# Zeros beside the last 64 keys' values, and two heads in every step, in a top-k attention, feed-forward and expert kernel

## The chip, the cores and the metric

The kernel runs on one NeuronCore of a Trainium2 chip. The metric is device time in microseconds (us): the median of several executions, beside one execution that the hardware profiler recorded. The engines are TensorE (PE; its weight loads are listed as PEld), VectorE (DVE), ScalarE (ACT), GpSimd (POOL) and SyncE (SP, which issues most DMAs).

## What is computed

Three layers, one after the other. The attention has 4 batches, 8 heads, 576 keys and head size 64; of each row of scores the 32 largest are kept. Its output, 2304 tokens of 512 values, passes a gated feed-forward layer (width 1536) and then a layer of 8 experts (width 1024), where every token goes to one expert.

```python
scores = scale * np.matmul(q, k.transpose(0, 1, 3, 2))
kth = np.partition(scores, -top_k, axis=-1)[..., -top_k:-top_k + 1]
scores = np.where(scores >= kth, scores, -1000000000.0)
attn = np.exp(scores - np.max(scores, axis=-1, keepdims=True))
attn = attn / (np.sum(attn, axis=-1, keepdims=True) + 1e-09)
x = np.matmul(attn, v)                        # heads side by side: 2304 x 512
xn = x / rms * rms_g                          # the feed-forward layer
x = silu(xn @ w_gate) * (xn @ w_val) @ w_out
out[mask] = gate_w[mask] * (relu(x[mask] @ w1[e]) @ w2[e])   # the experts
```

## The kernel before

**Tiles and steps.** The 576 queries and keys of a head are four chunks of 128 and a remainder of 64 (`SM` is 512, `SR` is 64). A tile is 128 rows of queries against all 576 keys: a main tile is one chunk of one head, a remainder tile holds 64 queries each of two heads. With 8 heads, 4 batches, 4 chunks and the remainders that is 128 main tiles and 16 remainder tiles. Two tiles make a step, and `main_steps` (L78) and `rem_steps` (L87) say which two; there are 72 steps. `PLAN` (L93) lists the chunks in order; only its entry `[0, 1]`, for the third batch, makes steps of two chunks.

**The path of a tile.** `dma_q`, `split_q` and `trans_q` bring in the queries: each value is split into a high and a low part on POOL (L456, L457), transposed on PE (L465) and copied to `qS`. `dma_k`, `split_k`, `trans_k` do the same for keys, once for a pair of heads, into `kS`. `qk` (L521) forms the scores on PE (L530); ACT copies them (L543); `topk` finds the 32nd largest on DVE with MAX8 and MATCH_REPLACE8 (L565, L568), after DVE has split each row into pairwise maxima and minima (L545, L546). `soft0` to `soft3` make the exponentials on POOL and ACT (L586, L595, L599, L603). `tr` (L616) transposes them on PE (L625) into `pT`; for the two tiles' last 64 keys together one more transpose (L630) makes `pr`, whose rows 0 to 63 belong to the step's first tile and rows 64 to 127 to its second.

**Values.** `dma_v` (L381) loads a pair of heads into `vt`: four chunks of 128 rows, and the last 64 keys twice, into the upper and the lower half of the rows (L388). `split_v` makes two 16-bit parts of it, `vs`, on ACT, DVE and POOL (L394 to L396). Of the first batch's second half of heads (`WHOLE`) the values stay 32-bit. `av` (L651) multiplies on PE (L671). A main tile in 16 bits takes 12 products with 128 rows (four chunks, three products each: high by high, high by low, low by high) and then 3 with 64 rows, the half of `pr` and of `vt` that belongs to this tile (`r0`). A remainder tile goes through this twice, once for each head in it, with 64 columns of exponentials each (12 products of 128 rows by 64 columns, then 3 of 64 by 64). ACT writes the result, scaled, to `xn` (L680).

```python
            r0 = i % 2 * SR
            parts = [(0, 128, hh)] if hh is not None else [(0, 64, 0), (64, 64, 1)]
            for o, n, h2 in parts:
                    ks = slice(0, 128) if c2 < CM else slice(r0, r0 + SR)
                nc.tensor.matmul(out=av_[o:o + n], lhsT=l, rhs=r, ...)
```

**The feed-forward layer** is cut into granules, one per 128 tokens (one granule has 256). A granule's matmuls are all at L750: 288 products into `pf` (gate and value half) and 72 into `po`, 6192 in all. `mlp_slot` (L1012) puts them, a few atoms at a time, into the seven slots of each attention step, so that PE has work while the attention waits; what is left over follows after the last step.

**The order on each engine** is fixed when the program is built: a scheduler in the framework places the instructions of the code above, with a priority for `tr`, `av` and `qk` (L1061 to L1067), and each engine then runs its list in order. The experts (L1109 on) begin after the last granule.

## Time and profile before

| what | value |
|---|---|
| median of 3 runs | 1242.8 us (1239.47 to 1243.44) |
| the profiled execution's own time | 1240.91 us |
| its span | 1239.3 us |
| PE busy | 1138.8 us, 92% |
| PEld busy | 1039.9 us, 84% |
| DVE busy | 928.2 us, 75% |
| ACT busy | 830.5 us, 67% |
| POOL busy | 731.2 us, 59% |
| mean granted TensorE clock | 0.937 |

All rows are from the profiled execution. The profiler models the end of a matmul, so matmuls overlap in it and a busy share of PE near 100% says only that no gap was long; how fast products follow each other is read from the starts of neighbouring rows. The attention's steps run from about 45 us to 833 us, the rest of the feed-forward layer to 928 us, the experts to the end.

### The profile page before, as it was taken

The page shows a single profiled execution, that of the slowest core. Times are in us where ns is not written, and L with a number is a line of the kernel's source. Part 1 is how long each engine was busy: PE and PEld are TensorE (multiplying, and loading weights), DVE is VectorE, ACT ScalarE, POOL GpSimd, SP SyncE. Part 2 cuts the span into 40 slices and gives each one's busy share as a digit, 9 for nine tenths or more (in the row PEclk, how much of TensorE's full clock was granted, in tenths as well). Part 3 has the DMA queues.
Part 4 walks back from the last instruction along what each step waited for, and adds up shares of the span by engine and source line. Part 5 has one row for each costly group of instructions (what it writes and reads, how often), then busy time and mean ns, then how long its engine had stood idle before and what let it go on. Part 6 is the DMA issues. An engine that isn't in the chain of part 4 may idle for free. (4 is left out here: it accounts for less than half of the span.)

```text
span 1239.3 us, 32187 instructions
## 1 busy us (share of the span) xinstructions
PE 1138.8 (92%) x12286; PEld 1039.9 (84%) x12286; DVE 928.2 (75%) x2886; ACT 830.5 (67%) x1757; POOL 731.2 (59%) x843
## 2 busy tenths in 40 slices
PE   6976677999999999999999999999997999999994
PEld 6965566888999989999998999999986898798883
DVE  8999999759999999998999999971125526244161
ACT  6868888777888888878888887873333435344260
POOL 7866766858767879867889676564434312222100
PEclk9865676989999999999999999999997999999997
DMA  8242312011000111000011000013006726354230
GB/s 295 51 129 82 100 44 82 13 45 39 21 17 9 32 41 47 24 13 15 17 38 40 28 17 2 11 32 124 11 19 193 247 70 230 128 173 149 66 113 20
DMA packets 69624, 87.54 MB, mean 71 GB/s; under 512 B 34626, under 2 KB 43974, under 8 KB 69448
## 3 DMA queue, kind: packets, MB, share of 16 engines
q1 hardware_dynamic: 62360, 67.86, 17.9%
q0 software_dynamic: 5424, 13.16, 3.3%
q10 hardware_dynamic: 1664, 4.19, 0.9%
q8 instruction: 107, 1.75, 0.6%
q14 instruction: 69, 0.57, 0.2%
HBM read 75.58 MB, written 10.92 MB: 70 GB/s over the span
## 5 line engine op out<-in xcount | busy, mean ns | idle before, releaser
L565 DVE MAX8 w<-w 128x8 f32<-128x296 f32 x576 | 251.9, 462 | 1.2
L599 POOL TENSOR_TENSOR s<-s,r 128x576 f32<-128x576 f32 x144 | 201.1, 1417 | 31.3 <-ACT r L595 31.1
L568 DVE MATCH_REPLACE8 w<-w 128x296 f32<-128x296 f32 x432 | 194.9, 455 | 0.0
L750 PE MATMUL pf<-xT,wg 128*128 128x128 f16 (+1 forms) x2448 | 172.0, 224 | 4.2 <-DVE T L879 2.6
L750 PE MATMUL pf<-xT,wv 128*128 128x128 f16 (+1 forms) x2448 | 167.7, 222 | 0.0
L750 PE MATMUL po<-wo,h 128*128 128x264 f16 (+1 forms) x1296 | 157.4, 275 | 0.9 <-ACT t L777 0.9
L530 PE MATMUL ps<-kS,qS 128*128 128x288 f32 x640 | 138.6, 346 | 20.7 <-DVE w L546 19.6
L750 PEld LDWEIGHTS <-wg 128*128 128x128 f16 x2448 | 148.3, 99 | 11.1 <-issue 4.9
L750 PEld LDWEIGHTS <-wv 128*128 128x128 f16 x2448 | 145.3, 98 | 4.3
L750 PEld LDWEIGHTS <-h 128*128 128x128 f16 x1296 | 122.0, 98 | 18.8 <-issue 1.4
L1137 DVE TENSOR_TENSOR wl<-wr,wh 128x1024 fp32r<-128x1024 f32 x64 | 76.7, 1220 | 66.1 <-ACT wh L1136 66.1
L530 PEld LDWEIGHTS ps<-kS,qS 128*128 128x128 f32 x640 | 104.0, 215 | 23.8 <-ACT r L595 14.9
L603 ACT ACTIVATE s<-s,mbs 128x576 f32<-128x576 f32 x144 | 113.3, 789 | 14.2 <-POOL s L599 13.9
L595 ACT ACTIVATE r<-s,mbs 128x576 f32<-128x576 f32 x144 | 105.0, 781 | 15.1 <-POOL mbs L586 15.0
L625 PE MATMUL pt<-identr,s 128*128 128x128 f32 x576 | 97.6, 300 | 16.9 <-ACT s L603 16.1
L543 ACT COPY s<-ps 128x576 f32<-128x576 f32 x144 | 93.1, 646 | 22.1 <-PE ps L530 21.5
L1243 POOL DMA_INDIRECT out_dram<-o,idx x23 | 23.2, 1010 | 138.0 <-ACT o L1242 106.9
L1184 PE MATMUL ph<-xh,wh 128*128 128x256 f32 x352 | 99.7, 287 | 1.0 <-PEq L1301 1.0
L1184 PE MATMUL ph<-xl,wh 128*128 128x256 f32 x352 | 98.5, 282 | 0.0
L1184 PE MATMUL ph<-xh,wl 128*128 128x256 f32 x352 | 97.1, 284 | 0.8 <-issue 0.8
L782 POOL TENSOR_TENSOR t<-u,t 128x512 f32<-128x512 f32 x54 | 69.6, 1289 | 47.9 <-ACT t L777 30.3
L671 PE MATMUL pt<-vs,pT 128*128 128x64 f16 (+1 forms) x1680 | 88.4, 198 | 8.7 <-POOL pT L639 6.7
(205 smaller groups left out, 2779.0 us busy)
## 6 DMA issues: line engine op xcount, KB each, us to landing
wr<-in_moe_w_dram SPq DMA_DIRECT2D x56, 512.0 KB
wst<-in_moe_w_gate_dram SPq DMA_DIRECT2D x24, 256.0 KB
wst<-in_moe_w_val_dram SPq DMA_DIRECT2D x24, 256.0 KB
kr<-in_k_dram SPq DMA_DIRECT2D x32, 128.0 KB
vt<-in_v_dram SPq DMA_DIRECT2D x32, 128.0 KB
x_d<-xo SPq DMA_DIRECT2D x16, 256.0 KB
wr<-in_moe_w_dram ACTq DMA_DIRECT2D x8, 512.0 KB
qr<-in_q_dram SPq DMA_DIRECT2D x112, 32.0 KB
```

Source lines behind the costliest of these rows:

```text
L530: nc.tensor.matmul(out=ps[:, a, 0:HS], lhsT=qS[i // 2][:, i % 2, j, o2:o2 + 128], rhs=kt[:, m, ks], start=(n == 0), stop=(n == len(ops) - 1),)
L543: nc.scalar.copy(out=s.rearrange("p (a k) -> p a k", a=2), in_=ps[:, :, 0:HS])
L565: steps.append(lambda: dve.max(lists[t][:, 8 * r:8 * r + 8], src[t] if r == 0 else dst[t]))
L568: steps.append(lambda: dve.match_replace(out=dst[t], in_to_replace=lists[t][:, 8 * r:8 * r + 8], in_values=src[t] if r == 0 else dst[t], i ...
L595: nc.scalar.activation(out=d["r"], in_=d["s"], func=AF.Relu, scale=-BIG, bias=d["mb"][:, 1:2])
L599: nc.gpsimd.tensor_tensor(out=d["s"], in0=d["s"], in1=d.pop("r"), op=OP.subtract)
L603: nc.scalar.activation(out=d["s"], in_=d["s"], func=AF.Exp, scale=SCALE, bias=d["mb"][:, 0:1], accum_out=d["rs"])
L625: nc.tensor.transpose(pt[:, c * 128:(c + 1) * 128], e[:, e0 + c * 128:e0 + (c + 1) * 128], ident)
L671: nc.tensor.matmul(out=av_[o:o + n], lhsT=l, rhs=r, start=(a == 0), stop=(a == len(ops) - 1))
L750: nc.tensor.matmul(out=out_, lhsT=l, rhs=r, start=(a == 0), stop=(a == len(ops) - 1))
L1137: nc.vector.tensor_tensor(out=lo, in0=w[0], in1=hi.bitcast(F32), op=OP.subtract)
L1184: nc.tensor.matmul(out=pt, lhsT=l[:, fs], rhs=r[:, kk, :], start=(n == 0), stop=(n == 3 * KD - 1))
```

## The change

- `dma_v` loads the last 64 keys of the pair's first head into rows 0 to 63 and of its second head into rows 64 to 127, once each; a POOL memset writes zeros into the other half (two memsets of 64x64 for each of 16 pairs; 32 DMAs of 64 for the last keys go).
- `av` uses all 128 rows for the last keys too: the other tile's rows of `pr` meet zeros. It also uses all 128 columns for a remainder tile, once per head, into two column ranges of the result (`m * D`), of which half the rows are read. The number of products stays.
- So that zeros meet the other tile, a step's two tiles must be the two heads of a pair. `main_steps` now makes steps so for the entry `[0, 1]` too (its eight steps' queries come in two DMAs in place of one), and a remainder tile now holds every second head: tile `hh` of a step has heads `2p + hh` and `2(p + 1) + hh`. `qk` takes the keys from two pairs for it.

```diff
@@ main_steps, rem_steps
-            if len(cs) == 2:
-                for hh in range(2):
-                    steps.append([(b, p, hh, c) for c in cs])
-            else:
-                steps.append([(b, p, hh, cs[0]) for hh in range(2)])
+            for c in cs:
+                steps.append([(b, p, hh, c) for hh in range(2)])
...
-            steps.append([(b, p, None, None), (b, p + 1, None, None)])
+            steps.append([(b, p, None, hh) for hh in range(2)])
@@ dma_v
+                nc.gpsimd.memset(vt[(1 - i) * SR:(2 - i) * SR, i, CM, :], 0.0)
                 nc.sync.dma_start(out=vt[:, i, 0:CM, :], in_=v[b, h, 0:SM, :].rearrange("(p c) d -> p c d", c=CM))
-                for j in range(2):
-                    nc.sync.dma_start(out=vt[j * SR:(j + 1) * SR, i, CM, :], in_=v[b, h, SM:S, :])
+                nc.sync.dma_start(out=vt[i * SR:(i + 1) * SR, i, CM, :], in_=v[b, h, SM:S, :])
@@ dma_q
-            if hh is not None and t1[2] == hh:
-                src = q[b, 2 * p + hh, 0:SM, :].rearrange("(p c) d -> p c d", c=CM)
-                nc.sync.dma_start(out=qr, in_=src[:, c:c + 2, :])
...
+                        nc.sync.dma_start(out=qr[i * SR:(i + 1) * SR, t, :], in_=q[b, 2 * (p + i) + c, SM:S, :])
@@ qk
-                ops = [(o2, m, j) for o2, m in ([(0, hh)] if hh is not None else [(0, 0), (64, 1)]) for j in range(2)]
+                ks_ = [(0, kS[b, p][:, hh, ks])] if hh is not None else [(64 * m, kS[b, p + m][:, c, ks]) for m in range(2)]
+                ops = [(o2, kt, j) for o2, kt in ks_ for j in range(2)]
@@ av
-            r0 = i % 2 * SR
...
-            parts = [(0, 128, hh)] if hh is not None else [(0, 64, 0), (64, 64, 1)]
+            parts = [(0, 128, p, hh)] if hh is not None else [(64 * m, 64, p + m, c) for m in range(2)]
...
-                    ks = slice(0, 128) if c2 < CM else slice(r0, r0 + SR)
-                    src, q0 = (pT, c2 * 128 + o) if c2 < CM else (pr, o)
-                    e = [src[ks, a, q0:q0 + n] for a in range(nh)]
+                    e = [pT[:, a, c2 * 128:(c2 + 1) * 128] if c2 < CM else pr[:, a] for a in range(nh)]
...
-                    nc.tensor.matmul(out=av_[o:o + n], lhsT=l, rhs=r, start=(a == 0), stop=(a == len(ops) - 1))
+                    nc.tensor.matmul(
+                        out=d["pt"][:, m * D:(m + 1) * D], lhsT=l, rhs=r, start=(a == 0), stop=(a == len(ops) - 1)
+                    )
```

The scheduler places everything anew, so rows move on all engines. Six lines fewer stand in the changed file, so L750 is L744 there, L671 is L663, L530 is L524, L625 is L619, L639 is L633.

On PE, where the second group of 48 feed-forward products (L750 before, L744 now; `wv` are the value half's weights) stands among the scores (`ps`), some 40 tiles into the program. Before:

```order
L530 MATMUL ps<-kS,qS 128x288 x8
L625 MATMUL pt<-identr,s 128x128 x4
L630 MATMUL sm<-identr,s 128x128
L425 MATMUL pk<-identr,ks 128x128
L671 MATMUL pt<-vt,pT 128x64 x8
L671 MATMUL pt<-vt,pr 128x64 x2
L465 MATMUL pq<-identr,qs 128x128 x4
L530 MATMUL ps<-kS,qS 128x288 x4
L421 MATMUL pk<-identr,ks 128x128 x4
L750 LDWEIGHTS wv_110
L750 MATMUL pf<-xT,wv_110 128x128
```

Now:

```order
L524 MATMUL ps<-kS,qS 128x288 x8
L619 MATMUL pt<-identr,s 128x128 x4
L421 MATMUL pk<-identr,ks 128x128 x4
L744 LDWEIGHTS wv_110
L744 MATMUL pf<-xT,wv_110 128x128
```

The feed-forward products stand ahead of one tile's scores and of one tile's products with the values that they followed before. The distance grows a little: by the 45th tile's scores 541 of the 6192 products at L744 have been listed, where 409 at L750 had been; at the last tile's scores it is 4832 and 4680; behind the last product with the values 1128 follow, where 1304 did (864 into `pf` in place of 1016, 264 into `po` in place of 288).

On PE, a remainder tile of the first batch among its products with the values. Before:

```order
L671 MATMUL pt<-vt,pr 64x64
L671 MATMUL pt<-vt,pT 64x64 x4
L671 MATMUL pt<-vt,pr 64x64 x2
L671 MATMUL pt<-vt,pT 64x64 x4
L671 MATMUL pt<-vt,pr 64x64
L425 MATMUL pk<-identr,ks 128x128
```

Now:

```order
L663 MATMUL pt<-vt,pr 128x64
L663 MATMUL pt<-vt,pT 128x64 x4
L663 MATMUL pt<-vt,pr 128x64 x2
L663 MATMUL pt<-vt,pT 128x64 x4
L663 MATMUL pt<-vt,pr 128x64
L524 MATMUL ps<-kS,qS 128x288 x4
```

The same number of products stands there, each now writing 128 rows of the result.

On POOL, early in the attention, where the scores minus the threshold (`s`), the splits of queries (`qs`) and values (`vs`) and the low parts of the exponentials (`pT`) follow each other. Before:

```order
L609 TENSOR_SCALAR sums<-sums 128x2
L639 TENSOR_TENSOR pT<-pf,pT 128x512
L586 TENSOR_TENSOR mbs<-w,cst_66 128x6
L639 TENSOR_TENSOR pT<-pf,pT 128x512
L599 TENSOR_TENSOR s<-s,r 128x576 x2
L456 TENSOR_TENSOR qs<-qr,zero 128x2x128
L396 TENSOR_TENSOR vs<-vt,vs 128x640
```

Now:

```order
L603 TENSOR_SCALAR sums<-sums 128x2
L386 MEMSET vt 64x64 x2
L633 TENSOR_TENSOR pT<-pf,pT 128x512
L580 TENSOR_TENSOR mbs<-w,cst_66 128x6
L633 TENSOR_TENSOR pT<-pf,pT 128x512
L593 TENSOR_TENSOR s<-s,r 128x576 x2
L396 TENSOR_TENSOR vs<-vt,vs 128x640
```

Two memsets of a pair's values stand in POOL's line, a few instructions ahead of the split that reads them.

## Rows read from the trace of the kernel before

**Rows 1.** The page: busy time by engine, and 40 equal slices of the span, in tenths.

```profile
PE 1138.8 (92%) x12286; PEld 1039.9 (84%) x12286; DVE 928.2 (75%) x2886; ACT 830.5 (67%) x1757; POOL 731.2 (59%) x843
...
DVE  8999999759999999998999999971125526244161
...
PEclk9865676989999999999999999999997999999997
```

**Rows 2.** Stretches: start:end, length, busy (count) by engine, granted clock, DMA share, GB/s.

```profile
60.00:150.00 90.00, 63.44 (x385) 54.29 (x385) 89.96 (x300) 70.87 (x150) 63.24 (x73) 0.61 0.37 105
150.00:280.00 130.00, 108.67 (x1072) 97.16 (x1072) 108.74 (x368) 102.15 (x227) 91.16 (x105) 0.81 0.17 47
280.00:833.50 553.50, 547.95 (x7435) 507.06 (x7433) 529.04 (x1803) 459.39 (x1026) 422.84 (x491) 1.00 0.09 24
833.50:927.50 94.00, 91.55 (x1328) 86.76 (x1327) 18.09 (x99) 30.01 (x60) 35.90 (x35) 1.00 0.15 50
927.50:1239.30 311.80, 280.17 (x1770) 249.08 (x1770) 130.85 (x191) 125.32 (x211) 68.94 (x70) 0.95 0.42 139
```

**Rows 3.** PE's longest waits, 280 to 833.5: total us, times, longest us.

```profile
PE pf L750 <- DVE u L772: 1.2, 1, 1.2
PE pf L750 <- DVE T L879: 1.0, 2, 0.6
```

**Rows 4.** DVE's longest wait in the same stretch.

```profile
DVE w L545 <- ACT s L543: 5.8, 14, 1.2
```

**Rows 5.** PE in order of time around a main tile: start, us, instruction, count.

```profile
412.79 0.72 PE L750 MATMUL pf<-xT,wg 128*128 128x128 f16 x10
413.35 0.51 PE L671 MATMUL pt<-vs,pT 128*128 128x64 f16 x12
413.80 0.26 PE L671 MATMUL pt<-vs,pr 64*128 64x64 f16 x3
413.99 0.29 PE L750 MATMUL pf<-xT,wg 128*128 128x128 f16 x2
```

**Rows 6.** Stretches, the matmuls of L671 alone: busy and count on PE, PEld.

```profile
280.00:833.50 553.50, 93.76 (x1770) 76.09 (x1770) 1.00 0.09 24
```

**Rows 7.** PE in order of time around a remainder tile.

```profile
371.55 0.57 PE L671 MATMUL pt<-vs,pT 128*64 128x64 f16 x12
372.05 0.28 PE L671 MATMUL pt<-vs,pr 64*64 64x64 f16 x3
372.25 0.56 PE L671 MATMUL pt<-vs,pT 128*64 128x64 f16 x12
372.75 0.28 PE L671 MATMUL pt<-vs,pr 64*64 64x64 f16 x3
372.96 0.40 PE L750 MATMUL pf<-xT,wg 128*128 128x128 f16 x4
```

**Rows 8.** PE in order of time: the last step's tiles, mixed, and a later feed-forward atom.

```profile
832.98 0.20 PE L671 MATMUL pt<-vs,pr 64*128 64x64 f16 x1
833.11 0.20 PE L671 MATMUL pt<-vs,pT 128*128 128x64 f16 x1
...
842.85 8.14 PE L750 MATMUL po<-wo,h 128*128 128x264 f16 x72 [0.30 <-ACT t L777]
```

**Rows 9.** A stretch with the clock low, and in it PE's feed-forward products.

```profile
257.00:268.00 11.00, 10.56 (x80) 9.14 (x81) 9.30 (x27) 9.46 (x24) 5.61 (x8) 0.54 0.22 60
...
264.65 3.64 PE L750 MATMUL pf<-xT,wg 128*128 128x128 f16 x32
```

**Rows 10.** POOL's memsets by form: count, busy us, mean ns, idle before.

```profile
L476 POOL MEMSET qS<- 128x256 f32 x8 | 2.5, 317 | 3.7 <-PE ps L530 3.7
...
L204 POOL MEMSET acc_oh<- 128x8 f16 x1 | 0.1, 105 | 0.1
```

**Rows 11.** SP's issues of the last keys' values (ns min/median/max), and a wait of SP.

```profile
L388 SPq DMA_DIRECT2D vt<-in_v_dram x64: 465/588/1630, 45.6 to 679.6; - x64
...
SPq L445 <- POOL qs L457: 128.9, 25, 11.1
```

More of the change, by code (lines that the diff above doesn't have):

```diff
@@ L435, in dma_q @@
             qr = ap_.tile([128, 2, D], F32, name="qr", tag="qr", bufs=QB)
-            t0, t1 = steps[s]
-            b, p, hh, c = t0
-            if hh is not None and t1[2] == hh:
-                src = q[b, 2 * p + hh, 0:SM, :].rearrange("(p c) d -> p c d", c=CM)
-                nc.sync.dma_start(out=qr, in_=src[:, c:c + 2, :])
-            else:
-                for t, (b, p, hh, c) in enumerate(steps[s]):
-                    if hh is not None:
-                        src = q[b, 2 * p + hh, 0:SM, :].rearrange("(p c) d -> p c d", c=CM)
-                        nc.sync.dma_start(out=qr[:, t, :], in_=src[:, c, :])
-                    else:
-                        for i in range(2):
-                            nc.sync.dma_start(out=qr[i * SR:(i + 1) * SR, t, :], in_=q[b, 2 * p + i, SM:S, :])
+            for t, (b, p, hh, c) in enumerate(steps[s]):
+                if hh is not None:
+                    src = q[b, 2 * p + hh, 0:SM, :].rearrange("(p c) d -> p c d", c=CM)
+                    nc.sync.dma_start(out=qr[:, t, :], in_=src[:, c, :])
+                else:
+                    for i in range(2):
+                        nc.sync.dma_start(out=qr[i * SR:(i + 1) * SR, t, :], in_=q[b, 2 * (p + i) + c, SM:S, :])
             raw["q", s] = qr
@@ L523, in qk @@
             ps = ps_s.tile([128, 2, 512], F32, name="ps", tag="s")
-            kt = kS[b, p]
             for a in range(2):
@@ L653, in av @@
             d = st[i]
-            pT, pr, av_ = d["pT"], d["pr"], d["pt"][:, 0:D]
-            r0 = i % 2 * SR
-            vt = vS[b, p]
+            pT, pr = d["pT"], d["pr"]
             nh = 1 if whole(b, p) else 2
-            parts = [(0, 128, hh)] if hh is not None else [(0, 64, 0), (64, 64, 1)]
-            for o, n, h2 in parts:
+            parts = [(0, 128, p, hh)] if hh is not None else [(64 * m, 64, p + m, c) for m in range(2)]
+            for m, (_, _, p2, h2) in enumerate(parts):
+                vt = vS[b, p2]
                 ops = []
                 for c2 in range(CM + 1):
-                    ks = slice(0, 128) if c2 < CM else slice(r0, r0 + SR)
-                    src, q0 = (pT, c2 * 128 + o) if c2 < CM else (pr, o)
-                    e = [src[ks, a, q0:q0 + n] for a in range(nh)]
+                    e = [pT[:, a, c2 * 128:(c2 + 1) * 128] if c2 < CM else pr[:, a] for a in range(nh)]
                     if nh == 1:
-                        ops.append((e[0], vt[ks, h2, c2, :]))
+                        ops.append((e[0], vt[:, h2, c2, :]))
                     else:
-                        w = [vt[ks, a, h2, c2, :] for a in range(nh)]
+                        w = [vt[:, a, h2, c2, :] for a in range(nh)]
                         ops += [(e[0], w[0]), (e[0], w[1]), (e[1], w[0])]
                 for a, (l, r) in enumerate(ops):
-                    nc.tensor.matmul(out=av_[o:o + n], lhsT=l, rhs=r, start=(a == 0), stop=(a == len(ops) - 1))
+                    nc.tensor.matmul(
+                        out=d["pt"][:, m * D:(m + 1) * D], lhsT=l, rhs=r, start=(a == 0), stop=(a == len(ops) - 1)
+                    )
             blk, x0 = (b * CM + c, 0) if hh is not None else (NMB + b // 2, (b % 2) * SR)
@@ L677, in post @@
             def post():
-                for o, n, h2 in parts:
-                    hd = 2 * p + h2
+                for m, (o, n, p2, h2) in enumerate(parts):
+                    hd = 2 * p2 + h2
                     nc.scalar.activation(
-                        out=x[x0:x0 + n, hd * D:(hd + 1) * D], in_=av_[o:o + n], func=AF.Copy,
+                        out=x[x0:x0 + n, hd * D:(hd + 1) * D], in_=d["pt"][o:o + n, m * D:(m + 1) * D], func=AF.Copy,
                         scale=d["rs"][o:o + n],
```

4 lines of the change are left out of this document (2 added, 2 removed).

## The prediction

> **What bounds the kernel now.** I read the page first, then a table of stretches, then the waits of PE and DVE in the longest of them, and at last PE's rows in order of time. PE is busiest over the whole run, but the slices of DVE are at 9 or more for most of the first two thirds and fall behind [rows 1]; so the run has parts with different limits. The table [rows 2] has five.
>
> - 60 to 150: DVE is busy 89.96 of 90.00 us. It is the bound; PE waits.
> - 150 to 280: DVE 108.74 and PE 108.67 of 130.00, at a granted clock of 0.81 on the mean. Neither is full.
> - 280 to 833.5: DVE 529.04 of 553.50, and the clock at its full level of 2.4 GHz (1.00). PE's longest wait here for anything is 1.2 us, its second 1.0 [rows 3], so PE issues practically all the time and bounds this stretch. DVE's 24.5 idle us are short waits for work that hangs on PE: the longest sum is 5.8 us in 14 pieces, for the copies of the scores [rows 4].
> - 833.5 to 927.5: feed-forward products alone. DVE is busy 18.09 of 94.00; PE is the bound.
> - The experts, 311.80 us, which the change does not touch.
>
> **The change part by part.**
>
> *The change of rows on PE.* Around a main tile the 12 products with 128 rows start at 413.35 and last 0.51 us in all. One alone is listed with 0.20 [rows 8], so eleven intervals take 0.31 to 0.32 (the rows are rounded) and one 0.029 us. At that pace the first product with 64 rows would start at 413.70; it starts at 413.80. The three with 64 rows last 0.26, so they too follow each other by about 0.03, the next other product would start at 413.89, and it starts at 413.99 [rows 5]. Each change between 128 and 64 rows thus costs 0.10 us, and two of them are in every tile: 0.64 us from the first product to the next instruction, where 15 x 0.029 = 0.44 would do. I take 0.20 us a main tile. A remainder tile runs from 371.55 to 372.96, 1.41 us, with 30 products that need 0.87 at the same pace; it saves 0.54 [rows 7]. In 280 to 833.5 there are 1770 products with the values [rows 6]; twelve remainder tiles (three batches' worth, of four) have 360 of them and the rest makes 94 main tiles: 94 x 0.20 + 12 x 0.54 = 25.3 us. The scheduler also mixes tiles, so that one product with 64 rows stands between others with 128 (832.98, 833.11 [rows 8]), each such piece paying both changes again. In the built order before, the products with the last keys stand in 209 separate runs, where unmixed tiles would have 160 (128 + 2 x 16). With a third more runs than tiles the sum is 25.3 x 209 / 160 = 33 us of PE's time in this stretch, which the new form doesn't need: all its products have 128 rows and columns.
>
> *What that is worth.* PE's need there falls from about 548 to about 515 us, while DVE's 529.04 busy us stay. Behind PE, DVE is next, and the stretch can shrink by 24.5 us at most; at least by nothing, if DVE's short waits are latencies of the chain and not PE's fault. In 60 to 150 DVE shows that it can run without a gap [rows 2], which speaks for the upper end; the copies it waits for also wait on ACT, busy 459.39, which speaks for the lower. I take the middle: **-12 us**, ends -24 and 0.
>
> *Feed-forward products ahead.* In the new order 1128 instead of 1304 feed-forward products stand behind the last product with the values. That is 152 fewer into `pf` and 24 fewer into `po`. In `pf` ten take 0.72 us and two 0.29, so eight intervals take 0.43 and one 0.054 us [rows 5]; in `po` 72 take 8.14, 0.111 each [rows 8]. The stretch behind the attention loses 152 x 0.054 + 24 x 0.111 = 8.2 + 2.7 = **-11 us**. These products were not saved but moved; 132 of them stand ahead of the 45th tile's scores already, that is before 280 us. There PE has 130.00 - 108.67 = 21 us free in 150 to 280 [rows 2]. 132 x 0.054 = 7.1 us fit in at the full clock; at the lower level of 1.2 GHz 32 products take 3.64 us, about 0.11 each [rows 9], and the 132 need 14.5. I take 0 for this stretch, with ends at -5 (row changes go here as well) and +15 (the products come ahead of scores that DVE waits for).
>
> *The memsets.* There are 32 of 64x64. Between the smallest, 105 ns for 128x8, and 317 ns for 128x256 [rows 10] I take 0.2 us, 6.4 us in all. They read nothing, so POOL doesn't wait in them, and POOL is busy 422.84 of 553.50 [rows 2]: it hides them. Without that cover they stand ahead of the threshold subtractions and cost up to 6.4 us. I take 0.
>
> *DMAs.* 32 of the 64 loads of last keys go, at 588 ns of SP's time each; eight loads of queries come. SP itself waits 128.9 us for POOL to free query buffers [rows 11], so its queue is ahead of need. Nothing. The remainder's scores need keys of two pairs at once; all pairs of a batch are loaded in its first four steps. Nothing. ACT's copies keep their number.
>
> The sum is -12 - 11 = -23 us. Against the profiled execution's 1240.9 that is 1218; the median of the runs stands 1.9 us above that execution, so I name **1219 us**.
>
> **A rule against the change.** The three products with 64 rows follow each other by about 0.03 us, as those with 128 rows do [rows 5]; two of them do not run at once. The sum above hence gives nothing up with them. The Trainium skill, "TensorEngine Tiling (Array Packing)", section Performance Considerations, recommends the opposite of this edit: for a contraction of 64 rows, tile the array twofold, since tiles work in parallel. By that rule two neighbouring tiles' last products would share their time and the edit would give up half of it. From the rows that is 0.03 x 3 / 2 = 0.045 us a main tile, about 5 us over 94 main tiles, and the time would be 1224. No row shows the overlap, so it stays inside the range.
>
> **The rivals.**
>
> 1. *DVE is a wall.* Its waits are latencies, the stretch 280 to 833.5 stays as long as it is although PE is freed, and only the shorter rest behind the attention counts: -11, **1231 us**. For it: DVE is busy 96% there [rows 2]. Against it: no idle time at all in 60 to 150. Chance 0.2.
> 2. *DVE closes up.* All of its 24.5 us go, and the early stretch gives its 5: -24 - 11 - 5 = -40, **1202 us**. For it: PE hardly waits [rows 3]. Against it: the mixture of latencies in DVE's waits. Chance 0.1.
> 3. *Slower: the early feed-forward products block the attention.* The 132 products run at the low clock ahead of scores, +15, and the memsets delay the threshold subtractions, +6; DVE, with only 24 us of slack in the whole rest, can't take that back, and the rest behind the attention is 11 shorter: +10, **1252 us**. It decides from the point where the early delay exceeds what the later stretches give back. For it: in 150 to 280, with the clock at 0.81, DVE is idle for 21 us and so already waits for others [rows 2]. Against it: PE has as much idle time there. Chance 0.07.
> 4. *The row count is not what costs.* If the 0.10 us come with the change of operands (from `pT` to `pr`), they stay, PE remains the bound to the end, and work moved ahead only changes place: **1242 us**, within 4. Against it: in rows 5 the next `pf` product pays the same on the way back, though it shares nothing with `pr`, and the change from `pf` to `pT` is free: ten times 0.054 after 412.79 is 413.33, and `pT` starts at 413.35. Chance 0.08.
>
> **How the numbers follow.** The forecast has 0.55. Its own range is 1209 to 1230. A measurement of this kernel can tell 0.3%, 3.7 us, from no change. Forecast and rivals 1 and 2 are all below 1239: faster 0.85. Rival 4 is the same: 0.08. Rival 3 is slower: 0.07. The range reaches from rival 2 to near rival 4, 1202 to 1238; outside lie half of rival 4 and rival 3, and something of the edges.
>
> **What would show it.** In the profile after, no product of `av` has 64 rows or columns, and from the first of a main tile's 15 products to the next instruction it takes 0.44 us and not 0.64. In the table of stretches PE has waits again between 280 us and the attention's end, on DVE's work, and DVE's share there rises above 96%. The attention ends about 12 us earlier, near 821, and some 83 us of feed-forward products follow where 94 did. If the 0.64 stays, the step on rows is wrong; if it falls and the attention ends at 833, rival 1; if the early stretch to the 45th tile is longer by over 10 us, rival 3.

## The result and the profile after

The median of the changed kernel is **1228.65 us** (1226.30 to 1230.71, 4 runs) against 1241.13 us for the kernel before in the same runs: a ratio of 0.9898, with a 95% interval of 0.987 to 0.9926. It is faster by 12.5 us. The forecast was 1219, with a range of 1202 to 1238: direction and range hold, and about half of the expected gain is there. The profiled execution after took 1229.35 us, with a span of 1227.6. Single executions of one kernel lie some us apart (the four after by 4.4), so a difference of a few us between stretches of two profiles is not told from that spread.

The page of the profile after, the lines that answer to [rows 1]:

```profile
PE 1107.4 (90%) x12286; PEld 1028.5 (84%) x12286; DVE 943.5 (77%) x2886; ACT 827.2 (67%) x1757; POOL 736.9 (60%) x875
...
DVE  7999999769999999999999999991234426344261
...
PEclk9855576999999999999999999999998999999997
```

PE is busy for 31 us less. DVE is busy for 15 us more, although it has the same 2886 operations. POOL has 32 operations more, the memsets.

The stretches after, in the columns of [rows 2]; the fourth ends with the last feed-forward product, and the last row begins with the 201st of the 640 score products, an event that both kernels have. The expectations below give its time as that of the 50th tile's scores; their counts of products ahead of the 50th tile's scores end one tile earlier, at the 197th score product, and those ahead of the 45th tile's at the 177th.

```profile
60.00:150.00 90.00, 63.65 (x378) 56.41 (x374) 88.21 (x294) 69.12 (x145) 60.62 (x70) 0.55 0.34 98
150.00:280.00 130.00, 107.03 (x1110) 100.34 (x1111) 112.99 (x360) 103.23 (x228) 94.06 (x113) 0.80 0.17 49
280.00:832.50 552.50, 530.11 (x7580) 501.73 (x7578) 542.81 (x1818) 461.75 (x1039) 433.28 (x517) 1.00 0.09 24
832.50:914.50 82.00, 79.76 (x1151) 75.50 (x1147) 16.79 (x98) 25.35 (x52) 29.91 (x29) 1.00 0.17 56
914.50:1227.60 313.10, 280.35 (x1770) 249.62 (x1770) 130.68 (x190) 125.19 (x211) 69.53 (x70) 0.95 0.42 138
...
305.30:832.50 527.20, 506.21 (x7241) 479.32 (x7242) 520.12 (x1750) 442.81 (x996) 410.99 (x490) 1.00 0.09 23
```

In the kernel before, the 201st score product starts at 296.7:

```profile
296.70:833.50 536.80, 531.61 (x7185) 491.96 (x7184) 514.52 (x1761) 444.64 (x996) 410.38 (x479) 1.00 0.09 24
```

Laid beside each other by events, the four parts are:

| part | before | after | difference |
|---|---|---|---|
| start to the 201st score product | 296.7 | 305.3 | +8.6 |
| from there to the end of the attention | 536.8 | 527.2 | -9.6 |
| feed-forward products alone | 94.0 | 82.0 | -12.0 |
| experts | 311.8 | 313.1 | +1.3 |
| sum, the difference of the spans | | | -11.7 |

In the second part PE has 506.21 busy us of 527.20, where it had 531.61 of 536.80. DVE has 520.12 of 527.20, so its idle time fell from 22.3 to 7.1 us. The end of the attention stayed where it was, at 832.5 against 833.5. The event that the prediction named for the early part, the 45th tile's scores with 541 and 409 products ahead of them, is the 181st score product: it starts at 274.4 us, where it started at 269.3, which is 5.0 us later.

PE in order of time around a main tile, after (columns of [rows 5]):

```profile
438.09 0.73 PE L744 MATMUL pf<-xT,wg 128*128 128x128 f16 x10
438.65 0.51 PE L663 MATMUL pt<-vs,pT 128*128 128x64 f16 x12
439.00 0.25 PE L663 MATMUL pt<-vs,pr 128*128 128x64 f16 x3
439.09 0.39 PE L744 MATMUL pf<-xT,wg 128*128 128x128 f16 x4
```

From 438.65 to 439.09 it is 0.44 us, where the tile of [rows 5] took 0.64. The three products with the last keys now follow the twelve at the common pace.

PE's longest waits after, 280 to 832.5 (columns of [rows 3]):

```profile
PE pt L663 <- DVE pT L635: 6.3, 9, 1.8
PE ps L524 <- DVE w L540: 4.8, 9, 1.4
PE pt L663 <- DVE pr L639: 1.8, 3, 0.9
```

And DVE's in the same stretch:

```profile
DVE w L539 <- ACT s L537: 2.9, 3, 2.2
```

The roles have changed: PE waits for DVE's results, up to 6.3 us for one kind where 1.2 was the most, and DVE's wait for the copies of the scores fell from 5.8 us [rows 4] to 2.9.

### The profile page after: what moved, and what is told of

The parts are those of the page before. It is cut to its first block, busy times and chain, and to the rows that moved or that the text cites. A ratio compares the mean times of both kernels' runs of the same rounds, so it can differ in the third digit from the quotient of the medians.

```text
span 1227.6 us, 32165 instructions
## 1 busy us (share of the span) xinstructions
PE 1107.4 (90%) x12286; PEld 1028.5 (84%) x12286; DVE 943.5 (77%) x2886; ACT 827.2 (67%) x1757; POOL 736.9 (60%) x875
## 5 line engine op out<-in xcount | busy, mean ns | idle before, releaser
L744 PE MATMUL pf<-xT,wv 128*128 128x128 f16 (+1 forms) x2448 | 169.8, 224 | 0.3 <-ACT xf L733 0.3
L744 PE MATMUL pf<-xT,wg 128*128 128x128 f16 (+1 forms) x2448 | 167.1, 222 | 2.5 <-ACT xT L730 1.4
L524 PE MATMUL ps<-kS,qS 128*128 128x288 f32 x640 | 141.1, 350 | 27.5 <-DVE w L540 24.5
L744 PE MATMUL po<-wo,h 128*128 128x264 f16 (+1 forms) x1296 | 157.8, 275 | 3.0 <-ACT t L771 2.4
L744 PEld LDWEIGHTS <-wv 128*128 128x128 f16 x2448 | 148.0, 99 | 5.2 <-issue 1.5
L744 PEld LDWEIGHTS <-wg 128*128 128x128 f16 x2448 | 146.6, 98 | 5.5 <-issue 1.6
L744 PEld LDWEIGHTS <-h 128*128 128x128 f16 x1296 | 122.6, 98 | 20.4 <-issue 3.3
L524 PEld LDWEIGHTS ps<-kS,qS 128*128 128x128 f32 x640 | 106.4, 219 | 32.3 <-ACT r L589 19.0
L1131 DVE TENSOR_TENSOR wl<-wr,wh 128x1024 fp32r<-128x1024 f32 x64 | 76.6, 1219 | 67.1 <-ACT wh L1130 67.1
L597 ACT ACTIVATE s<-s,mbs 128x576 f32<-128x576 f32 x144 | 113.9, 793 | 16.2 <-POOL s L593 15.8
L619 PE MATMUL pt<-identr,s 128*128 128x128 f32 x576 | 101.0, 306 | 15.0 <-ACT s L597 13.2
L663 PE MATMUL pt<-vs,pT 128*128 128x64 f16 x1680 | 79.3, 197 | 16.4 <-POOL pT L633 7.0
```

What stands on the lines that cost most here:

```text
L524: nc.tensor.matmul(out=ps[:, a, 0:HS], lhsT=qS[i // 2][:, i % 2, j, o2:o2 + 128], rhs=kt, start=(n == 0), stop=(n == len(ops) - 1),)
L597: nc.scalar.activation(out=d["s"], in_=d["s"], func=AF.Exp, scale=SCALE, bias=d["mb"][:, 0:1], accum_out=d["rs"])
L619: nc.tensor.transpose(pt[:, c * 128:(c + 1) * 128], e[:, e0 + c * 128:e0 + (c + 1) * 128], ident)
L663: nc.tensor.matmul(out=d["pt"][:, m * D:(m + 1) * D], lhsT=l, rhs=r, start=(a == 0), stop=(a == len(ops) - 1))
L744: nc.tensor.matmul(out=out_, lhsT=l, rhs=r, start=(a == 0), stop=(a == len(ops) - 1))
L1131: nc.vector.tensor_tensor(out=lo, in0=w[0], in1=hi.bitcast(F32), op=OP.subtract)
```

## The experiments

My theory after the result was: the removed row changes are worth what the prediction says of them, and about half is lost because the feed-forward products that moved ahead cost their full time early, where I had taken them as covered; in the middle DVE then sets the end. Rivals were that the pairing of heads does something by itself, that the memsets cost something, and that no engine but the chain of waits sets the end. Twelve kernels were run. The ratios below are to the kernel before in the same runs, with 95% intervals.

### The pairing alone

The changed kernel, with the last keys loaded twice again and products with 64 rows (and 64 columns for remainder tiles), no memset:

```diff
-                nc.gpsimd.memset(vt[(1 - i) * SR:(2 - i) * SR, i, CM, :], 0.0)
...
-                nc.sync.dma_start(out=vt[i * SR:(i + 1) * SR, i, CM, :], in_=v[b, h, SM:S, :])
+                for j in range(2):
+                    nc.sync.dma_start(out=vt[j * SR:(j + 1) * SR, i, CM, :], in_=v[b, h, SM:S, :])
...
+                    rs = slice(0, 128) if c2 < CM else slice(r0, r0 + SR)
+                    e = [pT[:, a, c2 * 128 + o:c2 * 128 + o + n] if c2 < CM else pr[rs, a, o:o + n] for a in range(nh)]
```

> The pairing of heads alone: steps, keys and queries as in the change, but the last keys' values loaded twice and multiplied on 64 rows (and 64 columns for a remainder tile), as before; no memset. In the built order the feed-forward products stand where they stood before (1304 behind the last product with the values). Theory (the rows of the last keys' products cost PE's time and the scheduler's order follows from them): the time of the kernel before, 1241 within 3 us; a main tile's 15 products keep 0.64 us. Rival (the pairing of two heads made the gain, through queries and keys): about 1229 us.

Measured: 1243.19 us, 0.9996 (0.9976 to 1.0015). PE in order of time, a main tile:

```profile
416.72 0.51 PE L666 MATMUL pt<-vs,pT 128*128 128x64 f16 x12
417.16 0.26 PE L666 MATMUL pt<-vs,pr 64*128 64x64 f16 x3
417.35 0.29 PE L745 MATMUL pf<-xT,wg 128*128 128x128 f16 x2
```

The tile takes 0.63 us again, and the whole gain is gone, as the expectation had it. No gain of the pairing by itself can be told; what counts is the rows, with the order that the scheduler makes of them.

### The memsets twice

```diff
                 nc.gpsimd.memset(vt[(1 - i) * SR:(2 - i) * SR, i, CM, :], 0.0)
+                nc.gpsimd.memset(vt[(1 - i) * SR:(2 - i) * SR, i, CM, :], 0.0)
```

> The change with each of its 32 memsets issued twice. The built order has 360 feed-forward products ahead of the 45th tile's scores, as before the change, where the change has 512, and 1152 in place of 1128 behind the last product with the values. Theory A (the 8.6 us that the change lost before the 50th tile come from the feed-forward products placed earlier): the 50th tile's scores start near 297 us again, not at 305, and the time is at or below the change's 1229. Theory B (they come from the memsets): the loss doubles, the 50th tile starts near 314 us, and the time is 3 to 9 us above the change's.

Measured: 1231.59 us, 0.9922 (0.9892 to 0.9951), which overlaps with the change's interval. One memset after takes 146 ns (the row of the line: count, ns min/median/max, first and last start):

```profile
L386 POOL MEMSET vt<- x32: 144/146/148, 46.6 to 672.5; 64x64 f32 x32
```

Thirty-two more of them, 4.7 us of POOL, make no difference that can be told: the time is 2.9 us above the change's, where the intervals overlap, and the 201st score product starts nowhere near the 314 us of theory B. Theory A had 297, and a time at or below 1229, and is missed by about 3 us in both. The added operations shifted the scheduler's order as well: 685 feed-forward products are recorded ahead of the 201st score product instead of 772, and the event is at 300.2, 5.1 us earlier; this run gives a point to the table below.

### More products in each slot, with and without the change

`MLP_SLOT` is the time in us that feed-forward products may fill in one of a step's seven slots. It is raised far, first after, then before:

```diff
-        MLP_SLOT = 1.3 if exact else 0.35
+        MLP_SLOT = 1.3 if exact else 1.0
```

> The change with the feed-forward budget of a slot at 1.0 in place of 0.35 (MLP_SLOT). The built order has 719 feed-forward products behind the last product with the values, not 1128. Theory (with full rows PE has room in the attention, VectorE is the bound there): the attention ends within 6 us of where it ended (832), what follows shrinks by 409 x 0.065 = 27 us, and the time is 1203 to 1210. Rival (PE is still full in the attention): the products only change place, 1226 to 1232.

> The kernel before with the same budget of 1.0; the built order has 719 feed-forward products behind the last product with the values, not 1304. Theory (PE bounds the attention's second part before the change, it has only some 5 us of waits between 280 and 833): the attention gets longer by nearly what the rest gets shorter (585 x 0.065 = 38 us), and the time stays within 10 us of 1241. Rival (VectorE bounds it before the change too): the attention ends at 833 and the time is about 1203.

Measured: 1275.37 us, 1.0264 (1.0229 to 1.0298), and 1306.18 us, 1.0507 (1.0472 to 1.0542). Both are slower by far, and the expectations missed: I had taken the moved products as covered again. The stretch from 280 us to the attention's end, first of the changed kernel with this edit:

```profile
280.00:902.50 622.50, 576.48 (x7885) 540.51 (x7884) 558.19 (x1861) 476.88 (x1064) 437.98 (x521) 0.96 0.08 20
```

And of the kernel before with it:

```profile
280.00:938.20 658.20, 620.74 (x7969) 565.77 (x7967) 552.15 (x1837) 479.16 (x1064) 438.80 (x508) 0.96 0.08 21
```

DVE now has 64 and 106 us without work. How the fuller slots make the attention 70 and 105 us longer was not taken apart; PE too is without work for 46 and 37 us of these stretches, so it is not full throughout. What the pair tells is the difference between them. The same number of products stands ahead of the 201st score product and behind the attention (1080 and 718 recorded in both), and the times differ by 30.8 us. That is near the 33 us of PE's time that the prediction counted for the row changes. Of the 30.8, 8 lie ahead of the 201st score product, which starts at 320.2 after and 328.2 before.

### DVE relieved of low parts

The prediction's limit for the middle was DVE. `PL1` sends, from tile 36 on, every second instead of every fourth tile's subtraction of low parts (`pT`) to POOL:

```diff
-        PL0, PL1 = 36, 4
+        PL0, PL1 = 36, 2
```

> The change with VectorE relieved: from tile 36 on every second tile's low parts of the exponentials are made on GpSimd, not every fourth (PL1 = 2), so 27 subtractions of 0.6 us leave VectorE, 27 of 1.2 us come to GpSimd and 27 copies of 0.6 us to ScalarE. Theory (with full rows VectorE is the wall of the attention's second part): the attention ends some 16 us earlier, near 816 to 822, and the time is 1212 to 1222. Rival (the attention's length is a chain of waits, or TensorE): it ends within 4 us of 832, 1225 to 1233.

> The kernel before with the same relief of VectorE (PL1 = 2). Theory (before the change TensorE bounds that stretch): the gain is small, the attention ends at 827 to 835, the time is 1234 to 1246. Rival (VectorE bounds it before the change as well): it gains the 16 us here too, about 1225.

Measured: 1237.0 us, 0.9968 (0.9953 to 0.9983) after, and 1249.08 us, 1.0056 (1.003 to 1.0083) before. They are worse by 8 and 7 us than without the edit, where the wall theory wanted the first one better. Both lie outside what theory and rival had: above 1233, and above 1246. The stretch from 280 us to the attention's end, after with this edit:

```profile
280.00:838.00 558.00, 528.55 (x7526) 498.91 (x7524) 538.56 (x1789) 471.84 (x1063) 458.20 (x541) 0.99 0.09 24
```

DVE lost 27 subtractions of some 0.67 us, 18 us, and its busy time in the stretch fell by 4.2 us only (542.81 to 538.56), while POOL's rose by 25 and the attention became 5.5 us longer. So DVE was hardly relieved, and the run does not say what a real relief would give. A third kernel puts more products into the slots:

```diff
-        PL0, PL1 = 36, 4
+        PL0, PL1 = 36, 2
...
-        MLP_SLOT = 1.3 if exact else 0.35
+        MLP_SLOT = 1.3 if exact else 0.42
```

> The change with VectorE relieved (PL1 = 2) and the feed-forward budget at 0.42 in place of 0.35, which leaves 1087 products behind the last product with the values (PL1 = 2 alone leaves 1152). Theory (TensorE has room again once VectorE is the wall): 65 x 0.065 = 4 us below the relief alone. Rival (products placed ahead of the attention's own delay it by as much, as with the budget of 1.0): the same time as the relief alone, or more.

Measured: 1226.88 us, 0.9877 (0.9849 to 0.9905). It is 10 us below the run with 0.35, with the attention's end unmoved (838.1 against 837.9): here the slightly fuller slots are covered. The expectation had 4 us for 65 products at 0.065; by the records all 65 are products into `po`, 7.2 us at the 0.111 of [rows 8].

### No feed-forward products in the first 22 steps, with and without the change

The direct test of the early part. `MS` keeps `mlp_slot` empty up to step 22:

```diff
-        MS, HP, HQ = 0, 500, 0
+        MS, HP, HQ = 22, 500, 0
```

> The change with the feed-forward budget held at 0 up to step 22 (MS = 22): 100 feed-forward products ahead of the 45th tile's scores instead of 512, and 1403 instead of 1128 behind the last product with the values. Theory A (feed-forward products placed early delay the attention): the 50th tile's scores start at 290 to 298 us, where the change has 305; behind the attention 275 x 0.065 = 18 us more follow; the time is 1230 to 1245. Rival (the early delay has nothing to do with them): the 50th tile starts at 303 us or later, and the time is 1243 to 1250.

> The kernel before with the feed-forward budget held at 0 up to step 22, as e8 did with the change. The two built orders place the feed-forward products nearly alike (339 and 333 ahead of the 50th tile's scores, 2412 and 2444 ahead of the 100th's, 1441 and 1403 behind the last product with the values), so the two differ in the rows of the last keys' products above all. Theory (in such an order TensorE's 33 us are the difference, part of them lost in waits): the stretch from the 50th tile's scores to the attention's end is 9 to 25 us longer than e8's 541, the time 1244 to 1262. Rival (other engines' waits set that stretch, with or without the change): it is within 5 us of 541, and the time 1236 to 1243.

Measured: 1235.91 us, 0.9954 (0.9938 to 0.997) after, and 1253.32 us, 1.0088 (1.0063 to 1.0113) before. From the 201st score product to the attention's end, and the feed-forward products behind it, after with this edit:

```profile
283.50:824.30 540.80, 519.00 (x7414) 488.87 (x7412) 526.00 (x1771) 446.55 (x1006) 416.16 (x497) 1.00 0.08 23
824.30:924.20 99.90, 97.15 (x1428) 92.28 (x1425) 19.59 (x107) 31.55 (x62) 39.26 (x37) 1.00 0.15 51
```

And before with it:

```profile
282.70:840.00 557.30, 546.16 (x7362) 503.56 (x7359) 522.49 (x1769) 448.73 (x1005) 414.01 (x480) 1.00 0.09 23
840.00:942.20 102.20, 99.38 (x1466) 94.52 (x1464) 19.94 (x110) 32.62 (x64) 39.76 (x38) 1.00 0.14 48
```

The 201st score product came earlier than theory A of the first had it (290 to 298); the rest fell as the two theories had it. Two things follow. With nearly the same products ahead (360 and 372 recorded) the 201st score product starts at 283.5 and 282.7: in such an order no gain of the rows shows in the early part. (With 1080 products ahead, in the slots of 1.0, it was 8 us.) And the middle is 16.5 us shorter with the change, the whole kernel 17.4 by the medians: that is what the rows are worth when the products stand alike. The early part itself begins to tell its price, with the records of feed-forward products alone up to that event (columns: start:end, length, busy and count of PE and PEld, clock, DMA share, GB/s). Before:

```profile
0.00:296.70 296.70, 47.25 (x656) 42.02 (x656) 0.79 0.31 91
```

After:

```profile
0.00:305.30 305.30, 57.50 (x772) 49.94 (x772) 0.77 0.30 89
```

After, with the first 22 steps empty:

```profile
0.00:283.60 283.60, 28.60 (x360) 23.72 (x360) 0.74 0.31 92
```

The records have a second thing to tell: products into `po` take 0.111 us at the full clock, twice the 0.054 of those into `pf` (both in the prediction). Those into `po` ahead of the event (columns: line, operation, count | busy us, mean ns | idle before), before:

```profile
L750 PE MATMUL po<-wo,h 128*128 128x264 f16 x44 | 5.8, 277 | 0.0
L750 PE MATMUL po<-wo,h 128*128 128x256 f16 x36 | 4.4, 273 | 0.0
```

After:

```profile
L744 PE MATMUL po<-wo,h 128*128 128x256 f16 x72 | 9.6, 273 | 0.0
L744 PE MATMUL po<-wo,h 128*128 128x264 f16 x72 | 9.6, 276 | 0.0
```

The same count of all kernels, those of the sections below among them:

| kernel | products ahead of the 201st score product | of them into `po` | it starts | attention ends |
|---|---|---|---|---|
| before, 22 steps empty | 372 | 72 | 282.7 | 840.0 |
| before | 656 | 80 | 296.7 | 833.5 |
| pairing alone | 656 | 80 | 300.5 | 836.9 |
| before, low parts on POOL | 668 | 92 | 302.1 | 842.6 |
| before, slot 1.0 | 1080 | 216 | 328.2 | 938.2 |
| after, 22 steps empty | 360 | 72 | 283.5 | 824.3 |
| after, scaling on ACT | 668 | 92 | 304.1 | 834.8 |
| after, memsets twice | 685 | 109 | 300.2 | 831.8 |
| after, test on POOL | 770 | 144 | 308.0 | 832.3 |
| after | 772 | 144 | 305.3 | 832.5 |
| after, low parts on POOL | 790 | 144 | 304.8 | 837.9 |
| after, slot 0.42 | 816 | 144 | 306.0 | 832.2 |
| after, low parts on POOL, slot 0.42 | 816 | 144 | 308.7 | 838.1 |
| after, slot 1.0 | 1080 | 216 | 320.2 | 902.5 |

Before, the 276 products into `pf` and 8 into `po` that the 22 empty steps take away need 15.8 us on PE at these paces, and the event comes 14.0 us earlier. After, 340 and 72 need 26.4 us, and it comes 21.8 us earlier. Most of that time shows, 89% and 83%. By the records it was longer, at a mean clock of 0.74 to 0.77: after, 57.50 and 28.60 busy us, 28.9 less, of which three quarters show. The 116 that the change's order has more are 52 into `pf` and 64 into `po`, 9.9 us, and at these shares they are worth 8.2 to 8.8 us, as much as the 8.6. But single kernels lie some us off such a sum. The pairing alone, with the products of the kernel before, has its event 3.8 us later than that; its granted clock from 60 to 150 us is 0.55, as after the change, where the kernel before has 0.61 [rows 2]. From the pairing alone to the change it is 4.8 us. The scaling on ACT has the event 7.4 us later than the kernel before with 12 products more, in an order of its own.

### The router's test on POOL, and the scaling of values on ACT

Two other reliefs of DVE. First the two operations of the router that test for finite numbers:

```diff
-            nc.vector.tensor_tensor(out=d, in0=L, in1=L, op=OP.subtract)
+            nc.gpsimd.tensor_tensor(out=d, in0=L, in1=L, op=OP.subtract)
...
-            nc.vector.tensor_scalar(out=d, in0=d, scalar1=0.0, scalar2=None, op0=OP.is_equal)
+            nc.gpsimd.tensor_scalar(out=d, in0=d, scalar1=0.0, scalar2=None, op0=OP.is_equal)
```

> The change with two small operations of the router per granule (the finite test, L841 and L842, 128x8 each) on GpSimd in place of VectorE; the built order of the feed-forward products stays (512 ahead of the 45th tile's scores, 1124 behind the last product with the values, where the change has 1128). In the profile after they take 0.14 to 1.45 us each on VectorE. Theory (VectorE is the wall of the stretch from 280 us to the attention's end): 24 of them less there, some 5 to 9 us, so the attention ends at 824 to 829 and the time is 1220 to 1226. Rival (a chain through all engines sets the length): it ends at 831 to 835, 1226 to 1232.

Then L395, which is 712 ns in the median:

```diff
-            nc.vector.tensor_scalar(out=vt, in0=vt, scalar1=SV, scalar2=None, op0=OP.mult)
+            nc.scalar.activation(out=vt, in_=vt, func=AF.Copy, scale=SV)
```

> The change with the scaling of the values (L395, 14 of 0.5 to 4.6 us) on ScalarE in place of VectorE. The built order has 360 feed-forward products ahead of the 45th tile's scores (the change 512) and 1172 behind the last product with the values (the change 1128). Theory (VectorE is the wall): 10 of them less after 280 us, some 9 us, and the early products block less, so the attention ends at 818 to 826; 3 us more follow; the time is 1218 to 1226. Rival (the chain through all engines, to which ScalarE's 14 operations add): the attention ends at 830 or later, 1228 to 1236.

Measured: 1227.45 us, 0.9863 (0.9837 to 0.9888), no difference to the change that can be told, with the attention's end at 832.3 against 832.5; and 1234.28 us, 0.9933 (0.9906 to 0.9959), worse by 6 us, with 1172 instead of 1128 products left behind the attention in the built order. So neither relief shortens the attention, as the rivals had it. Why the first does not is seen in DVE's groups from 280 us to the attention's end (line, operation, count | busy us, mean ns | idle before). The router's small operations before:

```profile
L882 DVE TENSOR_TENSOR T<-T,O 128x8 f32<-128x8 f32 (+1 forms) x12 | 8.6, 717 | 0.0
...
L855 DVE TENSOR_TENSOR O<-iota,mx 128x8 f16<-128x8 f32 (+1 forms) x12 | 3.3, 275 | 0.0
L843 DVE TENSOR_TENSOR T<-L,mx 128x8 f32<-128x8 f32 (+1 forms) x12 | 2.8, 237 | 0.0
L847 DVE TENSOR_TENSOR d<-L 128x8 f32<-128x8 f32 (+1 forms) x12 | 2.5, 206 | 0.0
...
L848 DVE TENSOR_SCALAR d<-d 128x8 f32<-128x8 f32 (+1 forms) x12 | 2.0, 166 | 0.0
```

After, six lines lower in number, in another order of size:

```profile
L841 DVE TENSOR_TENSOR d<-L 128x8 f32<-128x8 f32 (+1 forms) x12 | 6.0, 500 | 0.0
L849 DVE TENSOR_TENSOR O<-iota,mx 128x8 f16<-128x8 f32 (+1 forms) x12 | 5.7, 476 | 0.0
L876 DVE TENSOR_TENSOR T<-T,O 128x8 f32<-128x8 f32 (+1 forms) x12 | 4.9, 410 | 0.0
L837 DVE TENSOR_TENSOR T<-L,mx 128x8 f32<-128x8 f32 (+1 forms) x12 | 4.6, 386 | 0.0
L842 DVE TENSOR_SCALAR d<-d 128x8 f32<-128x8 f32 (+1 forms) x12 | 3.3, 271 | 0.0
```

And with the test on POOL:

```profile
L876 DVE TENSOR_TENSOR T<-T,O 128x8 f32<-128x8 f32 (+1 forms) x12 | 7.6, 637 | 0.0
L849 DVE TENSOR_TENSOR O<-iota,mx 128x8 f16<-128x8 f32 (+1 forms) x12 | 7.6, 631 | 0.0
```

The five groups take 19.2 us before and 24.5 after, for the same twelve operations each. With L841 and L842 gone from DVE (6.0 + 3.3 us), L849 and L876 grow by 4.6, and DVE's busy time in the stretch is 542.35 of 552.30 us, as it was (542.81 of 552.50). In part these operations have no length of their own, but take up a wait for POOL (the section on the hardware below); a busy share of DVE near 100% is therefore partly waiting. With more low parts on POOL (`PL1 = 2`) the five groups take 33.0 us. The stretch with the test on POOL, and the one with the scaling on ACT:

```profile
280.00:832.30 552.30, 532.24 (x7619) 503.57 (x7619) 542.35 (x1802) 465.81 (x1044) 440.20 (x542) 1.00 0.09 24
...
280.00:834.80 554.80, 530.84 (x7604) 499.89 (x7603) 534.73 (x1799) 460.63 (x1036) 428.62 (x512) 1.00 0.09 24
```

The scaling on ACT did take 8 us off DVE's busy time, and the attention still ended no earlier; but ACT got the work, and DVE waited 9.6 us for its copies of the scores, in place of 2.9.

### A little more in each slot, with the change

```diff
-        MLP_SLOT = 1.3 if exact else 0.35
+        MLP_SLOT = 1.3 if exact else 0.42
```

> The change with the feed-forward budget at 0.42 in place of 0.35: 1024 products behind the last product with the values (the change 1128), 788 ahead of the 50th tile's scores (the change 720). Theory (TensorE has some 17 us of waits in the attention that nothing used): 104 x 0.065 = 7 us off the rest, 68 x 0.053 = 4 us onto the start, the middle as long as it was: 1222 to 1229. Rival (the middle is as full as before, whatever waits show): it gets longer by as much, 1228 to 1233.

Measured: 1219.17 us, 0.9824 (0.9788 to 0.9861), the fastest of all, 9.5 us below the change and 3 below the theory's range. From the 201st score product on, and behind the attention:

```profile
306.00:832.20 526.20, 511.24 (x7301) 484.16 (x7302) 518.16 (x1768) 445.10 (x1002) 412.56 (x493) 1.00 0.08 23
832.20:905.60 73.40, 71.27 (x1045) 67.58 (x1041) 14.40 (x84) 22.37 (x44) 29.04 (x27) 1.00 0.18 61
```

The feed-forward products alone in the middle, with the edit and, below, without it:

```profile
306.00:832.20 526.20, 355.45 (x4355) 295.81 (x4356) 1.00 0.08 23
...
305.30:832.50 527.20, 346.00 (x4293) 290.49 (x4294) 1.00 0.09 23
```

Of the 104 products that no longer stand behind the attention, 62 by the records went into the middle (4355 in place of 4293). The middle is no longer for it (526.2 against 527.2), and PE's idle time there falls from 21.0 to 15.0 us. That is part of the room that the change left on PE, used. The kernel before with 0.42 was not run, so how much of the 9.5 us it would have given there is open.

## Why the prediction was right or wrong

- **The change of rows on PE: right.** 0.44 us in place of 0.64, and with 64 rows again 0.63. Rival 4 falls. The 33 us in all are borne out within a few us by the pair with slots of 1.0 (30.8 us of time, 8 of them in the early part).
- **What that is worth, -12 with ends -24 and 0: right, at about its size.** It measured -9.6, in part by luck: with products placed alike it is worth 16.5 us (the two kernels with 22 empty steps). By the records the middle has 98 products into `pf` more and 38 into `po` less than before, 1.1 us at their paces, so they do not make the difference; DVE had 34.8 us without work in that stretch there and 22.3 here, but what made it 9.6 is not shown. The bound that I named holds in one way: DVE's idle time closed up by 15 of 22 us, and PE has waits again. In another it does not: DVE's busy time did not stay at its value but grew by 5.6 us (514.52 to 520.12), so not all of what closed up became time. The router's five groups, 19.2 and 24.5 us from 280 us on, are about as much.
- **Feed-forward products ahead, -11: right.** 94.0 to 82.0 us, for 1304 and 1128 products.
- **"132 of them stand ahead of the 45th tile's scores already ... I take 0 for this stretch": the step that failed.** The stretch grew by 8.6 us to the 201st score product, and by 5.0 to the 45th tile's scores. That lies within the ends of -5 and +15 that stood beside the 0, nearer to +15. I had read PE's 21 us without work in 150 to 280 as room. It was not: PE is without work for 23 us of it after, and taking out most of the early products shortens the part by 89% and 83% of the time that they need at the full clock. Idle time that came from waits for results was no room there for work placed ahead of the scores. By that price the products can account for all of the 8.6 us, 64 of the 116 being the dear ones into `po`, where the prediction counted only the cheap ones. Against the pairing alone, which has the clock of the change there, the stretch grew by 4.8, so the rest may also be the clock.
- **The memsets, 0: right**, with 146 ns in place of the 0.2 us assumed, and doubled without an effect. The DMAs and ACT's copies were not tested by themselves; the pairing alone, which has the change's loads of queries, costs nothing that can be told.
- **"Two of them do not run at once": right for the tile that was read, wrong for the kernel.** Within a tile the products with 64 rows keep 0.03 us. In 31 places of the kernel before two of them start 3 to 8 ns apart (the section on the hardware). Of these 16 lie behind 280 us, half a us at 0.03 each, so the sum stands. That estimate's 0.045 us for 94 main tiles come to 4.2 us, not 5.
- **The sum** is one us off: 1240.9 - 23 + 1.9 is 1220.
- **Rival 3** had the right mechanism and its place, but it decides for slower only from the point where the early delay exceeds what comes later, and 8.6 us do not exceed 21.6. **Rival 1** named almost the time, 1231, and the end of the attention, 833, but by other parts: the stretch from the 201st score product did get shorter by 9.6, and the early part took it away. The sign that the prediction gave for it, the 0.64 gone and the attention's end at 833, came true and misleads: it cannot tell a middle that stays as long from a shorter one that begins later.

By the steps, the forecast of -23 became -11.7 by +8.6 (early), +2.4 (middle), -1.0 (behind the attention) and +1.3 (experts).

What stays open: which wait sets the length of the middle after the change. 62 more products on PE did not lengthen it, so PE's work does not set it. Three reliefs of DVE did not shorten it, but all three gave the work to POOL or ACT: two left DVE's busy time nearly as it was, and with the third DVE waited longer for ACT. A relief that loads neither was not run, so a limit by DVE, with the time that POOL blocks it, is not excluded, and the chain through PE, ACT, DVE and POOL in the order that the scheduler placed was not taken apart further. Also open are the 3.8 us by which the pairing alone is late at the 201st score product with products placed as before, at the lower clock. Its profiled execution, 1246.18 us, is 3 us above its median, so they may be no more than a difference between executions.

## What to carry to other kernels

When a change of the sums on one engine lets a scheduler place other work elsewhere, price the moved work, kind by kind, at nearly its full time where it now stands, and count idle time as room only if a run with more or less work in it says so: ahead of the scores it was none here, in the middle it was. Of a saving on the busiest engine expect what the next one leaves, and then fill the new gaps by hand: a slightly fuller slot gave 9.5 us here, a much fuller one cost 47. Half-filled products beside full ones can be dearer than full ones with zeros, if each change of shape is paid.

## What the runs showed of the hardware

**A DVE operation on 8 elements a row can take nine times its usual length beside POOL.** DVE in order of time after, at 592 us (columns of [rows 5]):

```profile
592.48 1.42 DVE L841 TENSOR_TENSOR d<-L 128x8 f32<-128x8 f32 x1
```

POOL in the same two us:

```profile
592.43 2.80 POOL L593 TENSOR_TENSOR s<-s,r 128x576 f32<-128x576 f32 x2 [0.62 <-ACT r L589]
```

L841 is 158 ns in the median and 135 at least, yet 1.42 us here: as long as one of POOL's two operations, during which it runs. It is not alone. Of the 85 operations of the five groups above in a whole trace, 15 take more than 250 ns in the trace before, 22 after and 32 with `PL1 = 2`, and every one of these ends 19 to 33 ns behind the end of an operation of POOL. The trace lists the wait as busy time. The Trainium skill, "SBUF — State Buffer", section "Who interferes with whom", says that a DVE instruction with two inputs in SBUF contends with a GpSimd instruction that reads SBUF, and that the one which comes second is blocked until the first ends; the trace agrees, with 1.42 us in place of 0.135. The prediction does not have it, though in the profile before such operations take 717 ns in the mean at L882.

**Products with 64 rows: one after the other in a tile, and sometimes two at once.** In the pairing alone three of one tile last 0.26 us, as in [rows 5], about 0.03 apart, and the change to 128 rows costs the 0.10 again. But the kernel before also has these (columns of [rows 5]):

```profile
296.51 0.23 PE L671 MATMUL pt<-vs,pr 64*128 64x64 f16 x2
...
297.64 0.20 PE L671 MATMUL pt<-vs,pr 64*128 64x64 f16 x2
```

The first two last 0.03 us longer than the 0.20 of one alone [rows 8]. The second two last as long as one: they start 4 ns apart. Of the 460 products with the last keys, 31 start 3 to 8 ns behind their neighbour in the kernel before, and none in less than 28 ns after the change. That such pairs belong to a step's two tiles, in different halves of the rows, is likely, but the rows don't name the half. The Trainium skill, "TensorEngine Tiling (Array Packing)", section Performance Considerations, advises two tiles of 64 rows for a contraction of 64, as the prediction says; the trace bears the overlap out in these places, and the change gives it up. It pays all the same, by 17.4 us with products placed alike: 31 of 460 overlap, while a change of rows at either end of a tile's last products costs 0.10 each time. An order that puts all last products of two tiles side by side was not run.
